# The last product of a decode step, in two column halves of 320 instead of four quarters of 160

## The chip, the cores and the metric

One core of one Trainium2 chip. The metric is device time in microseconds (us) of one execution; all runs below are of the state "fast" (none lies more than 1.5% above the fastest of the same kernel). A profile's times count from the start of the span, which is about 1.4 us shorter than the time of the same execution (660.0 us of span for 661.43 us of time).

## The reference, cut to what matters

```python
x = A_x                                                  # 4 rows of 640
h  = x + attention(layernorm(x), k_cache, v_cache, wq, wo)   # 32 heads, 4096 keys, cut here
h2 = h + mlp(layernorm(h), w1, b1, w2)

def mlp(x, w1, b1, w2):                                  # w1 640x1728, w2 1728x640
    a = x @ w1 + b1
    sp = log1p(exp(-abs(a))) + where(a > 0, a, 0)
    return (a * tanh(sp)) @ w2                           # the product that is changed
```

The caches, 4 x 32 x 4096 x 128 in bf16 each, are nearly all of the bytes. The MLP comes last, with w2 at its very end. What is changed is the product with w2, the addition of h to it, and the store of the 4 x 640 result.

## The kernel before: the parts that matter

Names: P = 128, D = 640, N = 4 rows, CG = 4 column tiles, QD = 32, OC = D // CG = 160, F = 1728 = 13 row blocks of 128 and a tail of 64 rows. `act` holds the activations, transposed, 4 columns to a row block. `mm` loads its own weights, `mm_same` multiplies with the weights already loaded. `pe.need(...)` waits for a result, or a load, of that name. A column tile is a product whose 4 output rows have a group of 32 PSUM partitions to themselves, so that several such products can run side by side.

```python
y2_ps = red[:, 0, 0:OC]                 # one PSUM bank; quarter k on partitions 32k..32k+3

def store(p, h):                        # p: SyncE (h = 0) or ScalarE (h = 1)
    p.need("o_bf")
    for k in range(h, CG, 2):           # two stores per queue
        load(p, out_rows[:, k*OC:(k+1)*OC], o_bf[k*QD : k*QD+N, :], ("out", k), f"OUT{h}")
# ... cut
def busy(n):                            # filler: products with zeros that nobody reads
    for _ in range(n):
        mm(o_full[:, :], ident[:, :], zeros[:, 0:1].to_broadcast([P, 512]), True, True)
# ... cut: w1 products; their first 28 stream 64 columns (wd = WD), the others 4 (wd = 1)
pe.need("h_lo", "h_hi")                 # residual h as a high and a low bf16 part
for part in (h_hi, h_lo):
    for k in range(CG):
        for c in range(DC):             # 40 products of 32 columns
            mm(y2_ps[k*QD : k*QD+N, :]..., part[:, c, :], ident[:, k*QD:(k+1)*QD], False, False)
busy(4)
pe.need("act")
def w2_mm(j):
    for k in range(CG):                 # four column tiles side by side
        mm(y2_ps[k*QD : k*QD+N, :], act[0:rows, j, :], w2_sb[:, j, k*OC:(k+1)*OC] ..., False, j == FM-1,
           "y2" if done else None)
w2_mm(FM)                               # the tail first
for j0, j1 in zip(W2S, W2S[1:]):        # W2S = 0, 4, 8, 12, 13: one load each
    pe.need(("w2", j0))
    for j in range(j0, j1):
        w2_mm(j)
# VectorE, at the end:
dv.need("y2")
dv.do(lambda: v.tensor_copy(out=o_bf[:, :], in_=y2_ps), "o_bf", DV)     # 128x160 at once
```

The softmax here doesn't subtract the row's maximum and nothing guards it: scores larger than these inputs give would overflow.

## Time and profile before

| | |
|---|---|
| time, median of three runs | 661.67 us (661.51 to 661.71) |
| span of the profiled execution | 660.0 us |
| HBM read | 283.35 MB, 429 GB/s over the span |
| last w2 load of 640 KB freed its products | 657.23 us |
| end of the span after that | 2.8 us |

The page's slices and its line on the memory say what bounds the kernel. Each digit of the first line is the busy share of the 16 DMA engines in one fortieth of the span, in tenths, 9 being 90% or more.

```profile
DMA  9999999999999999999999999999999999999997
...
HBM read 283.35 MB, written 0.01 MB: 429 GB/s over the span
```

The loads run without a gap to the last slice. No step on an engine shortens the kernel unless it comes after the last load, or holds up a load. The chain of waits, from the end back, in columns of start, duration (us) and what:

```profile
642.29 14.90 DMA slotA<-in_B_w_dram
657.19 0.04 issue
657.23 0.65 PE red L730 x20
...
657.91 0.32 DVE o_bf L726
```

The 20 products are the last five row blocks, four column tiles each. The first 16 start when the last of the three w2 loads of 640 KB lands; "the last w2 load" below means this one. The very last row block has a small load of its own, 160 KB. Its four weight loads start only at 657.62, and in e6, whose end is the same, the trace names the wait:

```profile
657.50 0.09 PEld L732 LDWEIGHTS red<-slotA,act 128*4 128x4 bf16 x4 [0.16 <-DMA slotA<-in_B_w_dram]
```

The cast to bf16 follows the last product. The timeline of the same stretch (start, duration, engine, line, operation, output and inputs, count, and in brackets how long the engine sat idle before and what ended that):

```profile
654.32 0.22 DVE L719 SCALAR_TENSOR_TENSOR act<-tb,hm 128x56 bf16<-128x56 f32 x1
...
655.13 1.27 PE L730 MATMUL red<-slotA,act 128*4 128x160 bf16 x32
...
657.23 0.62 PE L730 MATMUL red<-slotA,act 128*4 128x160 bf16 x20 [0.83 <-DMA slotA<-in_B_w_dram]
657.91 0.32 DVE L726 CAST o_bf<-red 128x160 bf16<-128x160 f32 x1 [3.37 <-PE red L730]
658.26 0.65 SPq L263 DMA_DIRECT2D out_dram<-o_bf  x2
```

TensorE has done the eight row blocks that landed first at 655.13 + 1.27 = 656.40 and then waits 0.83 us. Last, the granted clock of TensorE (the share of full speed that the profile says it was given) in short windows; the columns are the window, its length, busy time of PE, PEld, DVE, ACT and POOL with counts, then clock, DMA share and GB/s:

```profile
653.00:653.50 0.50, 0.29 (x27) 0.27 (x11) 0.38 (x2) 0.25 (x1) 0.00 (x0) 0.87 1.04 412
...
656.00:656.50 0.50, 0.41 (x15) 0.07 (x4) 0.00 (x0) 0.00 (x0) 0.00 (x0) 0.50 0.38 146
656.50:657.00 0.50, 0.00 (x0) 0.00 (x0) 0.00 (x0) 0.00 (x0) 0.00 (x0) 0.71 0.30 87
657.00:657.50 0.50, 0.27 (x16) 0.23 (x16) 0.00 (x0) 0.00 (x0) 0.00 (x0) 1.00 0.02 8
```

A mean of 0.87 over 653.0 to 653.5 is a step from 1.0 to 0.5 at about 653.4 (0.74 of the window at 1.0 and the rest at 0.5 gives 0.87), and 0.71 is a step back to 1.0 at about 656.8. So the first eight row blocks ran at half clock, and the last five at full clock.

### The profile page before, as it was taken

Reading aid. Unit: us, or ns where it says so; the run is one execution under the profiler, and the core shown is the slowest. Engines: PE = TensorE matmul, PEld = TensorE weight load, DVE = VectorE, ACT = ScalarE, POOL = GpSimd, SP = SyncE. Lnnn points to the kernel's source line nnn. Section 1 sums busy time; section 2 is a strip of 40 time slices with the busy share of each in tenths; the row PEclk is TensorE's granted clock in tenths of the full one; section 3 lists DMA queues with packets and bytes.
Section 4 is the critical chain, followed back from the end, with each engine's and each line's share of the span. In section 5 each row is a group of like instructions: output and inputs, shape, how many; then the busy total and the mean of one; then the engine's idle time right before and its main releaser. Section 6 shows DMA issues by size and latency. Waiting matters only on the chain. (4 is left out here: it accounts for less than half of the span.)

```text
span 660.0 us, 4989 instructions
## 1 busy us (share of the span) xinstructions
PE 383.8 (58%) x2636; PEld 68.4 (10%) x1680; DVE 407.8 (62%) x257; ACT 40.7 (6%) x157; POOL 1.7 (0%) x12
## 2 busy tenths in 40 slices
PE   1255758457327595838307395838434757665877
PEld 0000100101101010101100010000110001010145
DVE  1087988386048778677219798749206688957612
ACT  0200000000000000000000000000000000000011
POOL 0000000000000000000000000000000000000000
PEclk9778787879659796869668887879876769796868
DMA  9999999999999999999999999999999999999997
GB/s 418 409 445 445 438 441 417 422 441 438 438 437 425 429 437 437 441 437 421 433 437 437 441 437 417 437 437 433 441 441 417 437 433 437 441 441 417 425 416 312
DMA packets 6954, 283.50 MB, mean 430 GB/s; under 512 B 857, under 2 KB 1184, under 8 KB 2208
## 3 DMA queue, kind: packets, MB, share of 16 engines
q1 hardware_dynamic: 6912, 283.35, 99.4%
q8 instruction: 7, 0.11, 0.1%
q14 instruction: 3, 0.02, 0.0%
q10 hardware_dynamic: 32, 0.01, 0.0%
HBM read 283.35 MB, written 0.01 MB: 429 GB/s over the span
## 5 line engine op out<-in xcount | busy, mean ns | idle before, releaser
L529 DVE TENSOR_TENSOR slotA<-slotA,q_bc 128x8192 bf16<-128x8192 bf16 x32 | 140.7, 4416 | 93.1 <-DMA slotA<-in_A_k_cache_dram 93.1
L529 DVE TENSOR_TENSOR slotB<-slotB,q_bc 128x8192 bf16<-128x8192 bf16 x32 | 140.7, 4418 | 18.4 <-DMA slotB<-in_A_k_cache_dram 18.4
L540 DVE TENSOR_REDUCE s_f<-red 128x64 f32<-128x1024 f32 x64 | 78.0, 1219 | 96.3 <-PE red L740 96.2
L740 PE MATMUL red<-slotA,ident 128*128 128x512 bf16 x480 | 135.8, 446 | 0.0
L740 PE MATMUL red<-slotB,ident 128*128 128x512 bf16 x480 | 126.1, 422 | 0.0
L730 PE MATMUL red<-slotA,ident 128*128 128x512 bf16 x32 | 14.7, 458 | 129.4 <-PEq L49 129.4
L730 PE MATMUL pv<-slotC,e 128*32 128x512 bf16 x768 | 51.9, 430 | 37.3 <-PEq L49 34.3
L730 PE MATMUL red<-slotB,ident 128*128 128x512 bf16 x32 | 14.2, 443 | 89.1 <-PEq L49 89.1
L406 ACT ACTIVATE ex<-s_f 128x64 bf16<-128x64 f32 x64 | 16.4, 256 | 513.3 <-DVE s_f L540 513.3
L554 DVE TENSOR_TENSOR e<-ex,hmask 128x512 bf16<-128x512 bf16 x64 | 39.8, 684 | 0.0
L730 PEld LDWEIGHTS pv<-slotC,e 128*32 128x32 bf16 x768 | 22.1, 106 | 95.4 <-issue 81.3
L730 PEld LDWEIGHTS red<-slotA,ident 128*128 128x128 bf16 x32 | 3.2, 99 | 198.0 <-issue 197.9
L730 PEld LDWEIGHTS red<-slotB,ident 128*128 128x128 bf16 x32 | 3.1, 98 | 171.1 <-issue 171.1
L730 PEld LDWEIGHTS o_ps<-pv_sb,selo 128*32 128x32 f32 x136 | 13.5, 109 | 62.6 <-issue 62.6
L730 PE MATMUL o_ps<-pv_sb,selo 128*32 128x128 f32 x136 | 18.0, 276 | 0.0
L730 PE MATMUL pv<-slotA,e 128*32 128x512 bf16 x256 | 14.5, 380 | 0.6 <-PEq L49 0.5
L416 ACT COPY pv_sb<-pv 128x512 f32<-128x512 f32 x16 | 9.4, 586 | 69.5 <-PE pv L730 69.5
L406 ACT ACTIVATION_READ_ACCUMULATOR ex<-s_f 128x1 f32 x64 | 11.9, 186 | 0.0
L730 PEld LDWEIGHTS pv<-slotA,e 128*32 128x32 bf16 x256 | 6.9, 97 | 23.6 <-issue 17.8
L579 DVE RECIPROCAL rl<-misc 32x1 f32<-32x1 f32 x4 | 0.6, 150 | 12.6 <-PE misc L730 12.6
L519 DVE CAST b1T<-pv 128x13 bf16<-128x13 f32 x1 | 0.2, 174 | 12.1 <-PE pv L730 12.1
L730 PE MATMUL y_ps<-a_t,slotB 128*128 128x64 bf16 x160 | 7.3, 211 | 0.0
(107 smaller groups left out, 69.2 us busy)
## 6 DMA issues: line engine op xcount, KB each, us to landing
slotC<-in_A_v_cache_dram SPq DMA_DIRECT2D x2, 4096.0 KB, 42.2
slotC<-in_A_wq_dram SPq DMA_DIRECT2D x1, 5120.0 KB, 15.4
slotB<-in_A_wo_dram SPq DMA_DIRECT2D x3, 1280.0 KB, 15.4
slotA<-in_B_w_dram SPq DMA_DIRECT2D x3, 640.0 KB, 13.9
slotB<-in_B_w_dram SPq DMA_DIRECT2D x2, 864.0 KB, 22.1
slotB<-in_A_wo_dram SPq DMA_DIRECT2D x1, 640.0 KB, 19.0
slotB<-in_A_wo_dram SPq DMA_DIRECT2D x1, 480.0 KB, 19.8
slotB<-in_B_w_dram SPq DMA_DIRECT2D x1, 432.0 KB, 22.8
```

The costliest lines, as they stand in the source:

```text
L406: lambda: a.activation(out=ex[:, sl], in_=s_f[:, sl], func=ACT.Exp, scale=SCALE, accum_out=rs[:, b, s : s + 1],),
L416: lambda: a.copy(out=pv_sb[:, :, :].rearrange("p r d -> p (r d)"), in_=pv[:, :]),
L519: dv.do(lambda: v.tensor_copy(out=b1T[:, 0:FM], in_=b1_ps[:, 0:FM]), "b1m", DV)
L529: lambda: v.tensor_tensor(out=t, in0=t, in1=q_bc[:, hg, b, :].unsqueeze(1).to_broadcast([P, RS, Dh]), op=ALU.mult,),
L540: lambda: v.tensor_reduce(out=s_f[:, s * RS : (s + 1) * RS], in_=red[:, k : k + 2, :].rearrange("p k (r c) -> p (k r) c", c=CW), axis=AX.X ...
L554: lambda: v.tensor_tensor(out=e[:, sl, :], in0=ex[:, sl].unsqueeze(2).to_broadcast([P, RS, G]), in1=hmask[:, :].unsqueeze(1).to_broadcast( ...
L579: dv.do(lambda: v.reciprocal(out=rl[:, :], in_=l_ps), ("rl", hg), DV)
L730: lambda: nc.tensor.matmul(out_, lhsT=lhsT, rhs=rhs, start=start, stop=stop, skip_group_check=skip),
L740: return t.add_instruction(mybir.InstMatmult(name=nc.get_next_instruction_name(), engine=mybir.EngineType.PE, ins=[t.lower_ap(rhs), t.lowe ...
```

## The change

Intent: half as many products in the last stretch, one store per queue instead of two, the cast shared by VectorE and ScalarE, a residual without the high and low parts, and no filler. Its core, cut:

```diff
-    OC = D // CG
+    KO = 2
+    OC = D // KO
-    y2_ps = red[:, 0, 0:OC]
+    y2_ps = red[:, 0:KO, 0:OC]
     def store(p, h):
-        p.need("o_bf")
-        for k in range(h, CG, 2):
-            load(p, out_rows[:, k * OC : (k + 1) * OC], o_bf[k * QD : k * QD + N, :], ...)
+        p.need(("o_bf", h))
+        load(p, out_rows[:, h * OC : (h + 1) * OC], o_bf[h * QD : h * QD + N, :], ...)
 # ... ScalarE
+        ac.need(("y2", 1))
+        ac.do(lambda: a.copy(out=o_bf[QD : QD + N, :], in_=y2_ps[QD : QD + N, 1, :]), ("o_bf", 1), "AC")
 # ... VectorE: h_hi and h_lo go
-        dv.need("y2")
-        dv.do(lambda: v.tensor_copy(out=o_bf[:, :], in_=y2_ps), "o_bf", DV)
+        dv.need(("y2", 0))
+        dv.do(lambda: v.tensor_copy(out=o_bf[0:N, :], in_=y2_ps[0:N, 0, :]), ("o_bf", 0), DV)
 # ... TensorE
-        pe.need("h_lo", "h_hi")
-        for part in (h_hi, h_lo):
-            for k in range(CG):
-                for c in range(DC):
-                    mm(..., part[:, c, :], ident[:, k * QD : (k + 1) * QD], False, False)
-        busy(4)
+        pe.need("st", "ident_f")
+        for c in range(DC):
+            for k in range(KO):
+                mm(..., st[:, c, :], ident_f[:, k * P // KO : (k + 1) * P // KO], False, False)
         pe.need("act")
         def w2_mm(j):
-            for k in range(CG):
+            for k in range(KO):
                 cs = slice(k * OC, (k + 1) * OC)
-                mm(y2_ps[k * QD : k * QD + N, :], act[0:rows, j, :], ...)
+                mm(y2_ps[k * QD : k * QD + N, k, :], act[0:rows, j, :], ...)
 # ... cut: zero fill of the second bank, weights kept between neighbouring filler and bias
 #     products, Pool writes ident_f, the fp32 copy of the identity
```

More of the change, by code (lines that the diff above doesn't have):

```diff
@@ L196 @@
     ones_d = sb("ones_d", (P, P), FP32, tail, topA)
-    zeros = sb("zeros", (P, OC), BF16, tail, topA)
+    zeros = sb("zeros", (P, 1), BF16, tail, topA)
+    ident_f = sb("ident_f", (P, P), FP32, tail, topA)
     ysum = sb("ysum", (P, N), FP32, tail, topA)
@@ L210 @@
     b1_lo = sb("b1_lo", (P, FC, N), BF16, tail, topA)
-    h_hi = sb("h_hi", (P, DC, N), BF16, tail, topA)
-    h_lo = sb("h_lo", (P, DC, N), BF16, tail, topA)
     act = sb("act", (P, FC, N), BF16, tail, topA)
@@ L265, in store @@
     def store(p, h):
-        p.need("o_bf")
-        for k in range(h, CG, 2):
-            load(
-                p, out_rows[:, k * OC : (k + 1) * OC], o_bf[k * QD : k * QD + N, :],
-                ("out", k), f"OUT{h}",
-            )
+        p.need(("o_bf", h))
+        load(
+            p, out_rows[:, h * OC : (h + 1) * OC], o_bf[h * QD : h * QD + N, :],
+            ("out", h), f"OUT{h}",
+        )
     def leave(p, h):
@@ L276, in leave @@
             p.eng.sem_inc(fin, 1)
-            p.eng.wait_ge(o, 32).then_inc(o, -32)
+            p.eng.wait_ge(o, 16).then_inc(o, -16)
     def clear():
@@ L368, in pool_prog @@
         po.do(lambda: g.memset(zeros[:, :], 0.0), "zeros", "PO")
+        po.do(lambda: g.tensor_copy(out=ident_f[:, :], in_=ident[:, :]), "ident_f", "PO")
     def act_prog():
@@ L441, in act_prog @@
             "ta", "AC",
+        )
+        ac.need(("y2", 1))
+        ac.do(
+            lambda: a.copy(out=o_bf[QD : QD + N, :], in_=y2_ps[QD : QD + N, 1, :]), ("o_bf", 1), "AC"
         )
@@ L664, in dve_prog @@
         )
-        dv.do(lambda: v.tensor_copy(out=h_hi[:, :, :], in_=st[:, :, :]), "h_hi", DV)
         dv.need("std2")
@@ L676, in dve_prog @@
         dv.do(lambda: v.reciprocal(out=rstd[:, :], in_=std2[:, :]), "rstd", DV)
-        dv.need("h_hi")
-        dv.do(
-            lambda: v.tensor_tensor(
-                out=h_lo[:, :, :], in0=st[:, :, :], in1=h_hi[:, :, :], op=ALU.subtract
-            ),
-            "h_lo", DV,
-        )
         dv.need("b1_hi")
@@ L734, in mm, with mm_same @@
         )
-    def mm_same(out_, lhsT, rhs, start, stop, mark=None):
+    def mm_same(out_, lhsT, rhs, start, stop, mark=None, skip=True):
         t = nc.tensor
@@ L746, in emit @@
                     tile_size=(P, P), tile_position=(0, 0), ldweights=False,
+                    bass_skip_group_check=skip,
                 )
@@ L808, in fold @@
                 )
-                mm(*args, skip=False) if first else mm_same(*args)
+                (mm if first else mm_same)(*args, skip=False)
     def pv_mm(i):
@@ L886, in busy @@
         def busy(n):
-            for _ in range(n):
-                mm(o_full[:, :], ident[:, :], zeros[:, 0:1].to_broadcast([P, 512]), True, True)
+            for k in range(n):
+                (mm_same if k else mm)(
+                    o_full[:, :], ident[:, :], zeros[:, :].to_broadcast([P, 512]), True, True
+                )
         hg = NHG - 1
@@ L897, in pe_tail @@
         pe.need("zeros", ("e", NT - 1, NS - 1))
-        for k in (2, 3):
-            mm(red[:, k, :], ident[:, :], zeros[:, 0:1].to_broadcast([P, 512]), True, False)
-        mm(y2_ps, ident[:, :], zeros[:, 0:OC], True, False)
+        for k, w in enumerate((OC, OC, 512, 512)):
+            (mm_same if k else mm)(
+                red[:, k, 0:w], ident[:, :], zeros[:, :].to_broadcast([P, w]), True, False
+            )
         wo_mm(2)
@@ L912, in pe_tail @@
                 pe.need("b1_lo")
-                for part in (b1_hi, b1_lo):
+                for n, part in enumerate((b1_hi, b1_lo)):
                     for j0, j1 in ((0, FC // 2 + 1), (FC // 2 + 1, FC)):
-                        mm(h1_ps[:, j0:j1, :], ident[:, :], part[:, j0:j1, :], False, False)
+                        (mm_same if n or j0 else mm)(
+                            h1_ps[:, j0:j1, :], ident[:, :], part[:, j0:j1, :], False, False
+                        )
             pe.need(("w1", c0))
@@ L931, in pe_tail @@
                     )
-        pe.need("h_lo", "h_hi")
-        for part in (h_hi, h_lo):
-            for k in range(CG):
-                for c in range(DC):
-                    mm(
-                        y2_ps[k * QD : k * QD + N, :].rearrange("b (m c) -> b c m", c=DC)[:, c, :],
-                        part[:, c, :], ident[:, k * QD : (k + 1) * QD], False, False,
-                    )
-        busy(4)
+        pe.need("st", "ident_f")
+        for c in range(DC):
+            for k in range(KO):
+                mm(
+                    y2_ps[k * QD : k * QD + N, k, :].rearrange("b (m c) -> b c m", c=DC)[:, c, :],
+                    st[:, c, :], ident_f[:, k * P // KO : (k + 1) * P // KO], False, False,
+                )
         pe.need("act")
@@ L944, in w2_mm @@
             rows = P if j < FM else FT
-            for k in range(CG):
+            for k in range(KO):
                 cs = slice(k * OC, (k + 1) * OC)
-                done = j == FM - 1 and k == CG - 1
                 mm(
-                    y2_ps[k * QD : k * QD + N, :], act[0:rows, j, :],
+                    y2_ps[k * QD : k * QD + N, k, :], act[0:rows, j, :],
                     w2_sb[:, j, cs] if j < FM else w2_tail[0:FT, cs], False, j == FM - 1,
-                    "y2" if done else None,
+                    ("y2", k) if j == FM - 1 else None,
                 )
```

## The prediction

> **What bounds the kernel now.** The DMA queue. The page's slices show the DMA engines busy 90% or more in all slices but the last: 283.4 MB at 429 GB/s over 660.0 us. The change touches no load. The chain of waits and the timeline end so: last w2 load lands 657.19, 20 w2 products (five row blocks of 4 x 160 columns) 657.23 to 657.86, VectorE cast of 128x160 657.91 to 658.23 (324 ns), two stores per queue 658.26 to 658.91 (302 ns each), end 660.0. Narrow windows show the store traffic at 659.0-659.2 and 659.3-659.5, one burst per store. Only the 2.8 us (0.4%) after 657.2 can move the time; earlier blocks are done at 656.4, 0.8 us before the last load.
>
> **What the change does, costed.**
> 1. w2 products: four column tiles of 160 become two of 320. In the timeline the four products of a block run side by side: at half clock a block takes 133 ns (160/1.2 GHz). The Trainium skill, "TensorE: Matmul & The Clock Gate", Part 3, states this overlap of column tiles; the trace agrees. Two tiles take twice as long: 133 ns a block at full clock, 267 at half. [...] Estimate for the last five: 0.84 us at full clock, 1.5 at half, against 0.63 now.
> 2. The filler products (busy(4), 653.4-654.98) go. The granted clock falls to 0.5 at 653.4 and returns to 1.0 at 656.8, just ahead of the last load: one window of about 3.4 us that filler and w2 products filled. The same page, Part 1, states windows of this length; elsewhere in this trace, windows at half clock with a stream share of 0.63 to 0.75 did not bring the clock back, 0.88 did. Without the filler I estimate 0.63. So I expect clock 0.5 in the last products: +0.85 us. The first w2 product can start 0.3 us earlier (act is done 654.54, the product starts 654.90), in slack.
> 3. Cast: 320 columns instead of 160, VectorE beside ScalarE. VectorE from PSUM costs 1.04 ns a column here (160: 324 ns; 1024: 1219): 490 ns. ScalarE (128x512: 586; 128x56: 249): about 445. +0.17 us.
> 4. Stores: one per queue, not two: -0.3 us.
> 5. Residual: 40 bf16 products become 10 fp32 ones (20 passes), h_hi and h_lo (169, 149 ns) go; at 652.7-653.2, under VectorE's activation chain: off the path. The wider zero fill (+480 columns, 0.2 us at 643.6) and Pool's copy: off the path, in the wait for w1 at 650.2-650.8.
>
> Sum: +0.85 +0.17 -0.3 = about +0.7 us at half clock, +0.1 at full. I think half clock four times as likely.
>
> **Prediction: 662.2 us, range 661.4 to 662.9.** Chances: faster by over 2% 0.01, within 2% 0.98, slower 0.01.
>
> **What would show it.** Last w2 load still near 657.2; granted clock 0.5 from about 653 to the end; last ten products 1.4-1.5 us (0.8 if the clock is 1.0); cast 0.49 on VectorE beside 0.43-0.45 on ScalarE; a single store burst; end 2.8 to 3.5 us after the last load. Nothing in the loop changes.
>
> **What would make it wrong.** Column tiles that don't overlap (the earlier blocks then reach past 657.2: +3 us or more); an activation table load before ScalarE's copy (1.28 us); the loads landing differently by chance (0.3% is 2 us); a clock window that falls so that the last products run at full clock (a tie).

## The result, and the profile after

| | before | after |
|---|---|---|
| median of six runs, us | 661.56 (661.44 to 661.71) | 662.18 (662.08 to 662.42) |
| span of the profiled execution | 660.0 | 660.8 |
| TensorE free to start the last load's products | 657.23 | 657.10 |
| start of the cast | 657.91 | 658.90 |
| from the one to the other | 0.68 | 1.80 |
| from start of the cast to the end | 2.1 | 1.9 |

The ratio is 1.001, with an interval of 0.9997 to 1.0022: by the rule of 2% the same. The interval holds 1, but the two sets of six runs do not overlap: the slowest of before is 661.71, the fastest of after 662.08.

The chain of waits after has other members:

```profile
627.75 23.33 DMA slotB<-in_B_w_dram
...
651.13 1.18 PE red L726 x29
...
654.61 0.23 DVE act L715
654.83 0.04 issue
654.88 4.03 PE red L726 x28
658.91 0.47 DVE o_bf L722
```

The last w2 load no longer stands in it. It now starts from the load of w1 (slotB), goes through the w1 products and the activation on VectorE and ScalarE to `act`, and then through all 28 w2 products in one piece of 4.03 us. The timeline:

```profile
654.61 0.22 DVE L715 SCALAR_TENSOR_TENSOR act<-tb,hm 128x56 bf16<-128x56 f32 x1
...
655.24 3.63 PE L726 MATMUL red<-slotA,act 128*4 128x320 bf16 x26
657.10 1.16 PEld L726 LDWEIGHTS red<-slotA,act 128*4 128x4 bf16 x10 [0.17 <-DMA slotA<-in_B_w_dram]
658.90 0.48 DVE L722 CAST o_bf<-red 4x320 bf16<-4x320 f32 x1 [4.08 <-PE red L726]
658.93 0.42 ACT L445 CAST o_bf<-red 4x320 bf16<-4x320 f32 x1 [5.37 <-PE red L726]
659.38 0.28 ACTq L263 DMA_DIRECT2D out_dram<-o_bf  x1
659.41 0.30 SPq L263 DMA_DIRECT2D out_dram<-o_bf  x1
```

The 26 products of the whole blocks are one run without a pause. Only a weight load ahead of them waited 0.17 us for the last w2 load; the products themselves never did. The margin is small: the single records have the first product of that load starting at 657.32, 0.2 us after the load had freed it. The windows:

```profile
653.00:653.50 0.50, 0.50 (x15) 0.50 (x16) 0.41 (x2) 0.19 (x1) 0.00 (x0) 0.61 1.00 391
...
656.00:656.50 0.50, 0.50 (x6) 0.25 (x4) 0.00 (x0) 0.00 (x0) 0.00 (x0) 0.50 0.44 172
656.50:657.00 0.50, 0.50 (x6) 0.26 (x4) 0.00 (x0) 0.00 (x0) 0.00 (x0) 0.50 0.20 72
657.00:657.50 0.50, 0.50 (x6) 0.22 (x4) 0.00 (x0) 0.00 (x0) 0.00 (x0) 0.50 0.01 3
657.50:658.00 0.50, 0.50 (x8) 0.26 (x4) 0.00 (x0) 0.00 (x0) 0.00 (x0) 0.50 0.00 0
```

The clock drops at 653.1, as before at 653.4, and this time stays at 0.5. TensorE is busy all through. At this clock the row blocks start 0.267 us apart in the single records, twice the 133 ns that the prediction read in before's four column tiles. Thirteen of them, with 0.43 us (the shortest time of one product in this trace) for the last one, make 12 x 0.267 + 0.43 = 3.63 us, which is the duration in the timeline.

So the change costs 1.80 - 0.68 = 1.1 us between the last load and the cast, and gives back 0.2 us in cast and stores; the load came 0.1 us earlier in this execution. That is the 0.8 us of the spans, and 0.6 us in the medians.

### The profile page after: what moved, and what is told of

The parts are those of the page before. It is cut to its first block, busy times and chain, and to the rows that moved or that the text cites. A ratio compares the mean times of both kernels' runs of the same rounds, so it can differ in the third digit from the quotient of the medians.

```text
span 660.8 us, 4882 instructions
## 1 busy us (share of the span) xinstructions
PE 387.7 (59%) x2589; PEld 69.3 (10%) x1621; DVE 407.8 (62%) x255; ACT 41.1 (6%) x158; POOL 1.8 (0%) x13
## 5 line engine op out<-in xcount | busy, mean ns | idle before, releaser
L726 PE MATMUL pv<-slotC,e 128*32 128x512 bf16 x768 | 53.5, 440 | 37.4 <-PEq L49 34.4
L726 PE MATMUL red<-slotC,lnT 128*32 128x512 bf16 x40 | 4.5, 630 | 5.9 <-PEq L49 5.9
```

What stands on the lines that cost most here:

```text
L726: lambda: nc.tensor.matmul(out_, lhsT=lhsT, rhs=rhs, start=start, stop=stop, skip_group_check=skip),
```

## The experiments

Theory: the loss is the product of two parts of the change. Two column tiles take twice the time of four at the same clock, and without the filler this doubled time is spent at half clock. Rivals: the clock alone; the column tiles alone; the fp32 residual; the cast and the stores. Twelve runs of five rounds each, in three calls of four, each call on another chip with its own runs of before. All gave a correct result. Only the comparison with before is within the same rounds; after itself ran in the second call (e8). In the table "to cast" is the time from the weight load or product that the last w2 load freed to the start of the cast, "to end" from there to the end of the span, both from the one profiled execution, the end being that of the span before it is rounded to tenths; the clock is that of the last ten (or 20) products. The traced execution was the fastest of the five in e1, e3, e4, e6, e11 and e12, so a trace can look better than its median.

| run | median us (range) | before | difference | to cast | to end | clock |
|---|---|---|---|---|---|---|
| e1 after, filler back | 661.72 (661.35 to 662.53) | 661.43 | +0.29 | 0.88 | 1.9 | 1.0 |
| e2 before, no filler | 661.61 (661.38 to 662.07) | 661.43 | +0.18 | 0.89 | 2.1 | 0.5 |
| e3 after, four tiles | 661.77 (661.51 to 662.99) | 661.43 | +0.34 | 0.87 | 2.2 | 0.5 |
| e4 after, two stores per queue | 662.25 (661.95 to 662.86) | 661.43 | +0.82 | 1.08 | 2.2 | 0.5, 1.0 from 657.5 |
| e5 after, slower act | 662.53 (662.18 to 662.65) | 661.50 | +1.03 | no wait | 1.9 | 0.5 |
| e6 before, slower act | 661.44 (661.32 to 661.75) | 661.50 | -0.06 | 0.69 | 2.1 | 1.0 |
| e7 after, clock kept up | 661.37 (661.36 to 661.50) | 661.50 | -0.13 | 0.88 | 1.9 | 1.0 |
| e8 after again | 662.15 (661.57 to 662.36) | 661.50 | +0.65 | 1.55 | 1.9 | 0.5 |
| e9 after, bf16 residual | 661.78 (661.69 to 662.12) | 661.49 | +0.29 | 1.53 | 1.9 | 0.5 |
| e10 before, clock kept up | 661.45 (661.38 to 661.92) | 661.49 | -0.04 | 0.69 | 2.1 | 1.0 |
| e11 four tiles, clock kept up | 661.56 (661.45 to 662.00) | 661.49 | +0.07 | 0.67 | 2.2 | 1.0 |
| e12 as e7 | 661.46 (661.33 to 661.56) | 661.49 | -0.03 | 0.88 | 1.9 | 1.0 |

The 95% interval of every ratio but that of e4 (1.0001 to 1.0029) holds 1. A single difference of 0.3 us in the medians is therefore weak evidence.

### e1: the filler back in after

```diff
+        busy(2)
         pe.need("act")
```

> The kernel after with two filler products of 512 columns put back between the residual products and the w2 products. Theory (the lost clock made the loss): the filler and the w2 products fill one clock window, the clock goes back to 1.0 near 656.5 us of the span, the last products take 0.14 us a row block instead of 0.27 and end near 657.9 instead of 658.9: about 661.2 us, 1.0 less than after's 662.2. Rival (two column tiles are slower whatever the clock, or the cast and stores made the loss): the time stays at 662.2, or rises a little because the filler delays the products.

```profile
656.00:656.50 0.50, 0.50 (x10) 0.26 (x6) 0.00 (x0) 0.00 (x0) 0.00 (x0) 0.88 0.38 146
656.50:657.00 0.50, 0.34 (x6) 0.00 (x0) 0.00 (x0) 0.00 (x0) 0.00 (x0) 1.00 0.13 46
657.00:657.50 0.50, 0.36 (x6) 0.26 (x8) 0.00 (x0) 0.00 (x0) 0.00 (x0) 1.00 0.01 3
```

These are windows of e1. The clock came back at 656.1, TensorE was idle for a while again before the last load (busy 0.34 of 0.50), and the cast started 0.88 us after that load was in, not 1.80. In the profiled execution, 661.35 us, the theory holds. The median of 661.72 is 0.5 us above what I expected, and the runs spread over 1.2 us. Two filler products did not make every run fast. A reason was only argued: the step of the clock falls elsewhere in each execution, as shown under e4, and a filler that itself runs at half clock takes twice as long. Only one execution of e1 was traced.

### e2: before without its filler

```diff
-        busy(4)
         pe.need("act")
```

> The kernel before without its four filler products, nothing else. Theory: the clock stays at 0.5 to the end, but with four column tiles a row block takes only 0.13 us even so, so the last five end about 0.2 us later: 661.8 us against before's 661.6. The filler's loss alone is thus small; it is its product with the wider tiles that costs. Rival (the clock alone makes the loss): 662.2 us. Rival (filler useless): 661.6 or less.

```profile
657.01 0.84 PE L730 MATMUL red<-slotA,act 128*4 128x160 bf16 x20 [0.83 <-DMA slotA<-in_B_w_dram]
```

In this line of e2's timeline the last 20 products take 0.84 us at clock 0.5, against 0.62 at clock 1.0 in before, and the medians differ by 0.18. So the lost filler alone costs 0.2 us, not 0.6: with four column tiles TensorE is done early enough even at half clock, and waits 0.83 us for the last load as before.

### e3: after with four column tiles

```diff
-    KO = 2
+    KO = 4                            # 160 columns a tile, one PSUM bank again
 # ScalarE (k = 2, 3) and VectorE (k = 0, 1), two casts each into one half of the row:
-  a.copy(out=o_bf[QD : QD + N, :], in_=y2_ps[QD : QD + N, 1, :])
+  for k in (2, 3):
+      a.copy(out=o_bf[QD : QD + N, (k - 2) * OC : (k - 1) * OC], in_=y2_ps[k * QD : k * QD + N, :])
 # ... one store per queue stays; no filler, as in after
```

> The kernel after (no filler, fp32 residual, both casting engines, one store per queue) with the w2 products in four column tiles of 160 again, two casts of 4x160 on each engine into one half row. Theory: at clock 0.5 a row block takes 0.13 us instead of 0.27, the products no longer reach past the last load, and end about 0.85 us after it: near 658.0 instead of 658.9; casts about 0.5 us together as before. About 661.3 us. Rival (the activation chain, fp32 residual, cast or store make the loss): 662.2.

```profile
L729 DVE CAST o_bf<-red x2: 313/314/315, 658.0 to 658.3; 4x160 bf16<-4x160 f32 x2
L446 ACT CAST o_bf<-red x2: 284/285/286, 658.0 to 658.3; 4x160 bf16<-4x160 f32 x2
```

The products behaved as expected: at clock 0.5 they led to the cast in 0.87 us, as in e2, and 0.9 us sooner than in after. The cast did not: two casts of 4x160 on one engine do not overlap (durations in ns, minimum, median, maximum), 0.66 us on VectorE in place of the 0.5 I had put in, so the rest took 2.2 us and not 1.9. The span is 0.7 us shorter than after's, but the median only 0.3 us better relative to before; one of its five runs took 662.99 us, but its span was 660.6 us, so about 1 us of it lies outside the span; why is open. The number of column tiles alone thus takes away most of the loss at half clock.

### e4: after with two stores per queue

```diff
-        load(p, out_rows[:, h * OC : (h + 1) * OC], o_bf[h * QD : h * QD + N, :], ...)
+        for u in range(2):            # 160 columns each
+            load(p, out_rows[:, h * OC + lo : h * OC + hi], o_bf[h * QD : h * QD + N, lo:hi], ...)
```

> The kernel after with each half stored in two stores of 160 columns per queue, as many issues as before. Theory: the second issue, 0.3 us, comes on top and its data land 0.3 us later: 662.5 us, so one store per queue is worth 0.3 us. Rival (the end of the span does not hang on the number of stores): 662.2.

The end came 2.2 us after the start of the cast (a span of 660.45, less 658.22) instead of 1.9: the second store costs the expected 0.3 us. The median is 0.82 above before, after's 0.65. The trace gave something else as well:

```profile
654.00:654.50 0.50, 0.00 (x0) 0.00 (x0) 0.47 (x2) 0.00 (x0) 0.00 (x0) 0.60 0.98 389
...
657.50:658.00 0.50, 0.50 (x10) 0.23 (x6) 0.00 (x0) 0.00 (x0) 0.00 (x0) 0.98 0.00 0
```

Up to the store this kernel is after, without any filler. Yet here the clock fell at 654.1, not 653.1, and returned at 657.5, in the middle of the last products, so that they led to the cast in 1.08 us. The drops lie at 653.1, 654.1, 654.6 and 653.1 in the traces of after, e4, e5 and e8, whose TensorE work up to the w2 products is the same to within 0.3 us. The Trainium skill, "TensorE: Matmul & The Clock Gate", Part 1, says that the window is free-running and does not reset at the start of a kernel; these traces agree: drop and return are one window of 3.4 us apart here (654.1 to 657.5) and in before (653.4 to 656.8), and where the window begins differs from run to run. The window of e4, begun 1 us later than that of after, is filled with w2 products for longer (TensorE busy 2.78 of 3.40 us, against 2.60); that this brought the clock back is argued, not tried.

### e5 and e6: a slower activation, in after and in before

```diff
+        dv.do(lambda: v.reciprocal(out=tb3[:, :, :], in_=tb2[:, :, :]), "tb3a", DV)
+        dv.need("tb3a")
         dv.do(lambda: v.reciprocal(out=tb3[:, :, :], in_=tb2[:, :, :]), "tb3", DV)
```

> The kernel after with the reciprocal of the activation computed twice: 0.54 us more in the chain of VectorE that ends in act. Theory (in after, the products run without a pause from act to the end, so the chain w1 load, activation, 28 products is what ends last, and before's slack is gone): act about 0.54 us later, the end of the products and the kernel as much later: 662.6 to 662.7 us against after's 662.1. Rival (after still hangs on the last w2 load): no change, 662.1.

> The same second reciprocal in the kernel before. Theory: act comes at about 655.1 instead of 654.5; the filler ended at 655.0 anyway, and the blocks that landed early are done at about 656.6, still 0.5 us ahead of the last load: no change, 661.5 (less than 0.15 us). Rival (before is bound by the activation chain as well): 662.0.

The chain of waits of e5, then that of e6:

```profile
654.49 0.51 DVE tb L714
...
655.02 0.23 DVE act L717
655.25 0.04 issue
655.29 4.03 PE red L728 x28
659.33 0.47 DVE o_bf L724
```

```profile
642.25 14.82 DMA slotA<-in_B_w_dram
657.07 0.04 issue
657.11 0.67 PE red L732 x20
...
657.80 0.33 DVE o_bf L728
```

The same half microsecond costs 0.38 us in after (662.53 against 662.15 of e8, in the same rounds, though the ranges overlap) and nothing in before (-0.06). In e5's trace the piece of 4.03 us is as long as in after and moves with `act`, start and end; in e6's it is the last w2 load that ends the wait. So in after and e5 the bound of the last stretch has moved from the load to the activation chain; e8 and e9 show by how little. If after had still hung on the last load, e5 would have cost nothing; if before had hung on the activation too, e6 would have cost as much as e5.

### e7 and e12: after with the clock kept up

```diff
-                    wd = WD if c0 == 0 else 1
+                    wd = WD                      # all w1 products stream 64 columns
+            if c0 == W1S[1]:
+                busy(2)                          # in the wait for the second w1 load
             pe.need(("w1", c0))
 # ...
+        busy(3)
         pe.need("act")
```

> The kernel after with the clock kept up from earlier on: all w1 products stream 64 columns (only the first 28 did), two filler products in the wait for w1, three between residual and w2 products. Theory: the clock stays at 1.0 past 653, a w2 row block takes 0.14 us, the blocks that landed early end before 656.5, the last ten products end about 0.85 us after the last load: span about 659.9 and 661.4 to 661.7 us, as with the filler alone. If the clock falls all the same (fill too thin), the filler delays the products and it is 662.3 or more. Rival (the clock is not the cause): 662.1.

> The warm version of after once more, on this chip and in these rounds: 661.4 us, runs within 0.2 of each other, 0.1 below before.

The windows of e7:

```profile
653.00:653.50 0.50, 0.50 (x21) 0.39 (x13) 0.38 (x3) 0.25 (x1) 0.00 (x0) 1.00 0.97 381
...
656.50:657.00 0.50, 0.00 (x0) 0.00 (x0) 0.00 (x0) 0.00 (x0) 0.00 (x0) 1.00 0.16 59
657.00:657.50 0.50, 0.38 (x6) 0.27 (x8) 0.00 (x0) 0.00 (x0) 0.00 (x0) 1.00 0.02 8
```

And the line of e7's timeline that answers to the last of before:

```profile
657.12 0.84 PE L726 MATMUL red<-slotA,act 128*4 128x320 bf16 x10 [0.84 <-DMA slotA<-in_B_w_dram]
```

The clock stays at 1.0, TensorE waits for the last load again, and the ten products take 0.84 us, as predicted for full clock. The time is 661.37 us, 0.78 us under e8 in the same rounds, and the five runs lie within 0.14 us of each other where those of e8 span 0.79. e12, on the third chip, repeats it: 661.46 us, 0.03 under its before (expected: 0.1), its runs within 0.23. With the clock up, after is as fast as before: the loss sat in the half clock acting on two column tiles. The two tiles still take 0.2 us longer to the cast than before's four (0.88 against 0.69 in e6), and cast and stores give these 0.2 us back. The wider products and the two filler products were added together; which of the two holds the clock was not tried.

### e8: after again

> The kernel after, unchanged, on this chip and in these rounds, to compare the others with: 662.1 us, 0.6 above before. In its trace I look for where the step of the clock falls: if the steps come at fixed points of the kernel, the clock is 0.5 to the end again; if they run free of the kernel, the step of this trace lies elsewhere.

662.15 us, 0.65 above before. The drop of the clock lies at 653.1 and the clock is 0.5 to the end, as in the first trace. That the step runs free of the kernel thus shows in e4 and e5, not in this comparison. In another respect the two traces differ. The first w1 product after the wait starts at 650.91 here and at 651.13 in after, and so the w2 products start at 654.65 and not 654.88. The eight early row blocks are then done just as the last w2 load lands, and from there the cast is 1.55 us away, 0.87 more than in before. Of the five runs one took 661.57 us; it was not traced.

### e9: after with the bf16 residual

```diff
-        pe.need("st", "ident_f")
-        ... st[:, c, :], ident_f[:, k * P // KO : (k + 1) * P // KO]
+        pe.need("h_lo", "h_hi")
+        for part in (h_hi, h_lo):
+            ... part[:, c, :], ident[:, k * P // KO : (k + 1) * P // KO]
```

> The kernel after with the residual added as before, by bf16 products of a high and a low part (20 of 64 columns), with VectorE's two steps for them. Theory (the residual is off the path: TensorE is done with it 1 us before act): no change against after, 662.1 us, within the spread that the free step of the clock gives (661.6 to 662.4). Rival (the fp32 passes hold up the w2 products): 0.3 us or more less, 661.8.

Inconclusive by time: 661.78 us is where the rival put it, inside the range of e8, and on another chip. The trace does not bear the rival out. There the w2 products start with `act` and lead to the cast 1.53 us after the last load, in e8 1.55 us, and in after TensorE sat idle 0.80 us between the fp32 residual and `act`. (In e9 the last w2 load did hold the products a little: the 26 took 3.71 us, not 3.63.) The fp32 products therefore held nothing up in a traced execution; what the 0.37 us between the two medians are, I cannot say.

### e10 and e11: before with the clock kept up, and all in one

```diff
 # e10, on before: wd = WD for all w1 products, busy(2) in the wait for w1; its busy(4) stays
 # e11, on e3: the same, and busy(3) ahead of act
```

> The kernel before with the clock kept up (all w1 products 64 columns wide, two filler products in the wait for w1; its four filler products stay). Theory: before's last ten to twenty products ran at clock 1.0 in its trace anyway and cost 0.2 us more at the most in a run where the step falls badly: 661.4 us, 0 to 0.1 less than before, with runs closer together. Rival (a warm clock is worth as much to four tiles as to two): 660.8.

> Everything that helped in one: four column tiles, clock kept up, two casts of 4x160 on each engine, one store per queue. Estimate from the traces: products 0.65 us after the last load instead of 0.84, casts 0.66 instead of 0.48, the rest as in the warm version of after: 661.4 us, equal to the warm after within 0.1. If the casts of 160 overlap better, 661.2.

e10 is 0.04 us under before: four tiles gain nothing that can be seen from the clock. Its runs spread over 0.54 us, no closer together than before's nine (0.51), which I had expected otherwise. e11 does have the shortest products (0.67 us to the cast), and loses it again by its two casts in a row (2.2 us to the end). None of the combinations beats before by an amount that these runs can tell from zero.

## Why the prediction was right, point by point

- **What bounds the kernel.** Right for before: the DMA queue, and only what follows the last load counts. e6 shows the slack.
- **Time.** 662.2 predicted, 662.18 measured, range 661.4 to 662.9. This closeness is partly luck: five runs of after spread over 0.8 us in e8, and the terms were less exact than their sum.
- **Column tiles and clock.** Right: 0.267 us a row block at half clock, 0.84 us for the last ten products at full clock (e7), clock 0.5 to the end in four of the five traces of after and of its versions without filler and with two tiles (after, e5, e8, e9; in e4 it returned within the last products). The Trainium skill, "TensorE: Matmul & The Clock Gate", Part 3, states that column tiles run side by side; the 20 products of before in 0.62 us and the 0.84 of e7 show it here. Before's last five row blocks: the single records have the first four of them start 0.07 us apart and the fifth 0.18 us later, when its own load is in.
- **The step that failed.** "The first w2 product can start 0.3 us earlier (act is done 654.54, the product starts 654.90), in slack", and with it the sum that began at the last load. The sum holds only if the first eight row blocks are done when the load lands. In the first trace of after they were not: 28 products, 4.03 us from `act` on, ended at 658.9, and the last load was no longer what they waited for. There the term was 1.80 us to the cast, +1.1 us and not +0.85, and the tail 3.7 us, outside the 2.8 to 3.5 of the prediction. In e8 and e9, where `act` came 0.2 to 0.3 us earlier, the term was 1.55 and 1.53 us, +0.87 and +0.85, as predicted, and the tail 3.4 to 3.5 us. So the path was right within 0.3 us and the slack was nil: a later `act` does count, as e5 shows.
- **Cast.** Right: 479 ns on VectorE and 416 on ScalarE, against 490 and about 445. The Trainium skill, "TensorEngine Tiling (Array Packing)", PSUM Bottleneck, advises to use both engines to empty PSUM. Here it was slower with the split into two halves of 320 columns: VectorE alone had done all four quarters in 324 ns.
- **Stores.** Right: 0.3 us for the second one (e4). Cast and stores together gave back 0.2 us against the 0.13 predicted.
- **Residual, zero fill, Pool's copy.** Off the path in the traces. The times of e9 leave 0.37 us unexplained.

## What to carry to other kernels

Ahead of the last load of a memory-bound kernel, what keeps TensorE's clock up can be work that nobody reads; before taking a filler away, look at the clock in the window that its successors will run in. Halving the number of column tiles doubled the time of a row block at the same clock (133 to 267 ns at half clock) and spends slack that another stage was living on: sum the chain from its own start, here the activation, as well as from the last load. And a result that lies on several groups of partitions is cast in one instruction at the price of its columns, so trading partitions for columns makes the cast longer, even with two engines on it.

## What the Trainium skill lacked or had wrong

- "TensorE: Matmul & The Clock Gate", Part 1, gives the half clock as the state after an idle window. Here the clock fell after a window in which the trace counts TensorE busy 2.62 of 3.40 us (before, 650.0 to 653.4), most of its products streaming only 4 to 32 columns; and in after a window with 2.60 of 3.40 us busy (653.1 to 656.5) did not bring it back, where one with 2.92 did in before (653.4 to 656.8). The page names no share at which it turns, and these busy times don't settle one: the profile models the ends of products, so a window of narrow products looks busier than it is.
- "TensorEngine Tiling (Array Packing)", PSUM Bottleneck, advises both engines for emptying PSUM, and also to vectorize the access across tiles in one bank, without a figure for either. For this result of 4 rows the second did better: one VectorE cast of 128x160 took 324 ns; 4x320 on VectorE beside 4x320 on ScalarE took 479 and 416 ns; two of 4x160 on one engine took 0.66 us. Sharing the 160 columns of the one cast between both engines was not tried.
